# Cached attention of two blocks on one core: wq loaded in its own column order, and the permutation moved into VectorE's K transposes

## The chip, the core and the metric

The kernel runs on one core of a Trainium2 chip. The core has TensorE (PE in the profile), VectorE (DVE), ScalarE (ACT), GpSimd (POOL) and SyncE (SP), which run their own instruction streams and meet at semaphores, and sixteen DMA engines that move data between HBM and the on-chip memory SBUF. PSUM is the memory into which PE accumulates. The metric is the time of one execution in device microseconds; the runs of one kernel are told by their median.

## The reference

Two independent attention blocks, A and B, with the same shapes. Each projects x to queries, attends to a given cache of keys and values, and projects back; the two outputs stand side by side.

```python
B, Sq, D = 16, 64, 640
H, Sk, Dh = 32, 512, 128
q = (x @ wq).reshape(B, Sq, H, Dh).transpose(0, 2, 1, 3)
scores = einsum("bhqd,bhkd->bhqk", q, k_cache) * Dh ** -0.5
p = softmax(scores, axis=-1)
o = einsum("bhqk,bhkd->bhqd", p, v_cache)
out = o.transpose(0, 2, 1, 3).reshape(B, Sq, H * Dh) @ wo
```

All data are bf16. K and V are 67 MB each in a block and are read once; wq (640 x 4096) and wo (4096 x 640) are 5.2 MB each in a block.

## The kernel before

**Packs and phases.** The unit of work is a pack: 4 heads of 2 batches. A group is 4 packs (`NJ`), which share the same 2 batches and so the same x; 8 groups make a phase (32 packs), in which 16 heads go through all 16 batches. There are 4 phases: the two halves of the heads of block A, then of B; 128 packs in all. A phase needs half of a block's wq and wo: 640 x 2048 and 2048 x 640, 2.62 MB each.

**A pack n, in order of its data.** SP loads K (two DMAs of 512 KB, from pack 8 on, L631) into a ring of 6 packs and V (one of 1 MB, L641) into a ring of 4. VectorE transposes K in 32x32 blocks of 4-byte elements (KT, L702); a 4-byte element is a pair of bf16 values of neighbouring columns of a head. PE multiplies wq by x (QP, L688, 20 matmuls), ScalarE copies q (QE), PE makes the scores (S, L712), ScalarE the exponentials and their sums (EX, L741), VectorE the reciprocals (RC, L754), Pool scales (NM, four per pack, L762), PE transposes the weights (TR, L774), VectorE copies them out of PSUM (TE, L854), PE multiplies by V (PV, L867), ScalarE copies (OE), PE multiplies by wo (OP, L887). At a new group PE transposes x (XT), ScalarE copies it (XE), and Pool puts it into the one buffer that QP reads (XC, L677; in even phases also XS, L672).

**The order is planned.** `build_plan` makes a list of operations, each with its engine, a due time in units of packs (the table `AT`: QP of pack n is due at n - 0.428, S at n, and so on), and what it reads and writes. Each engine's program is its operations sorted by due time. SP's program is sorted by the times in `loads` instead. Waits follow from reads and writes: an operation waits for the last writer of what it reads, and a load for the last readers of what it overwrites. Engines run in order, so whatever stands behind a waiting operation waits too. PE's program and ScalarE's are loops, so a few waits are moved off PE: for instance QP's on its weights (where `op.kind == "QP"` in the patch-up loop, L263), and OP's on wo, which is put on the fourth NM of the pack before (L258).

**What sets SP's pace.** V of pack n goes where V of pack n - 4 was; SP takes as a sign that PV of pack n - 4 is done the TR of pack n - 3, which stands behind it on PE (`stand_in`, L294). K stands behind V in SP's order and mostly needs no wait of its own.

**wq.** Its load `LDWQ` brings, per phase, five pieces of 512 KB (one for each 128 rows; 128 partitions with runs of 4,096 bytes, L615) into a staging tile `ws_sb`. Pool copies them into `wqp_sb` with `WP` (L656), eight copies of 128 x 1280 per phase, two for each pack index j. The copies change the order of the columns: within each 512 columns pairs of columns from the two halves of a head are interleaved, so that q comes out with the head's columns in the order in which the K transpose lays K out. QP reads `wqp_sb[:, j]` in steps of four columns (`(c f) -> f c`, L685). As `ws_sb` is apart from `wqp_sb`, wq of the next phase can be loaded while this phase still computes: SP's list has the five loads for phase 1 among the first ones, and those for phases 2 and 3 spread over the phase before, 0.14 x 32 packs apart (L177). The second buffer costs 20 KB in each partition.

Of the kernel before, what the change touches and what calls it, by code (L numbers as in the profile page):

```python
# [20 lines left out]
class Cfg:  # L21
# [18 lines left out]
              TRH=(1.0, 1.05), TEH=(1.15, 1.2), TEX=1.2, PVH=(1.45, 1.46), OEH=(1.5, 1.55), OPY=(1.1, 1.57),  # L40
              OPZ=(1.65, 1.7), OSH=(1.75, 1.8), STH=(1.85, 1.9), FL1=1.3, FLM=1.68, FLC=1.82, WP0=(-1.6, -1.59, -0.7, -0.69, 0.25, 0.26, 1.25, 1.26),
              WP1=(-3.5, -2.55, -2.45, -1.5, -0.5, 0.5, 0.6, 1.5))

# [43 lines left out]
def build_plan(dims, cfg, general):  # L87
# [84 lines left out]
    for ph in range(NPH):  # L172
        twp = [ph * PH + t for t in AT["WP1" if ph else "WP0"]]
        for kt in range(dims["KT"]):
            ready = (twp[-1] - PH if ph > 1 else AT["WP0"][-1]) + 0.5
            op = add("sp", "LDWQ", (ph, kt), twp[0] - 0.5 if ph else -20.0, [], [("ws", kt, j) for j in range(NJ)])
            loads.append((ready + 2.0 + 0.14 * PH * kt if ph > 1 else AT["PV"] + 0.15 if ph else -50.0, 1, op))  # L177
        for j in range(NJ):
            w = ph * NJ + j
            n0 = ph * PH + j  # L180
            for i in range(2):
                add("pool", "WP", (w, i), twp[2 * j + i], [("ws", kt, j) for kt in range(dims["KT"])], [("wqp", j, i)])
            if ph:
                loads.append((n0 - NJ + AT["LDWO"], 4, add("sp", "LDWO", w, n0 + AT["OP"] - 0.8 * NJ, [], [("wo", j)])))
            else:
                loads.append((n0 - 1.9, 4, add("sp", "LDWO", w, n0 + AT["OP"] - 0.8 * NJ, [], [("wo", j)])))
# [6 lines left out]
    for n in range(-2, N):  # L193
# [3 lines left out]
        g, j = n // NJ, n % NJ  # L197
        add("pe", "QP", n, n + AT["QP"], [("xT", g % cfg.NX), ("wqp", j, 0), ("wqp", j, 1)], [("SB", 1)])
        add("act", "QE", n, n + AT["QE"], [], [("SB", 1), ("qs", n % cfg.NQ)])
# [53 lines left out]
    for op in ops:  # L253
# [6 lines left out]
        if op.kind == "XT" and op.idx > 0:  # L260
            at[("NM", 4 * (NJ * op.idx - NJ) + 3)].deps += [d for d in op.deps if d.kind == "LDX"]
            op.deps = [d for d in op.deps if d.kind != "LDX"]
        if op.kind == "QP" and op.idx > 0:  # L263
            op.deps = [d for d in op.deps if d.kind != "WP"]

# [15 lines left out]
    def stand_in(d, op):  # L281
# [12 lines left out]
        if d.kind == "PV" and op.eng == "sp":  # L294
            return at[("TR", d.idx + 1)]
        if d.kind == "QP" and op.eng == "pool":
            return at[("TR", d.idx - 1)]
# [28 lines left out]
    def sem_key(op):  # L326
        if op.kind == "LDX" and op.eng == "act":
            return ("d_first",) + op.writes[0]
        if op.kind == "LDV":
            return ("d_v" if op.idx[1] else "d_vh", op.writes[0][1])  # L330
        if op.kind in LOADS:
            return ("d_" + op.kind[2:].lower(),) + op.writes[0][1:]
        if op.kind in ("ST", "STH"):
            return ("d_out",)
        return ("q_" + op.eng,) if for_pe(op) else ("s_" + op.kind.lower() + "_" + op.eng,)
# [169 lines left out]
def mha_kernel(nc, blocks, out, cfg=None):  # L505
# [26 lines left out]
    with contextlib.ExitStack() as es:  # L532
# [4 lines left out]

        wqp_sb = sb("wqp_sb", [128, NJ, KT, 512], BF16)
        wo_sb = sb("wo_sb", [128, HPH, D], BF16)
        ws_sb = sb("ws_sb", [128, KT, NJ, 512], BF16)  # L540
        kn_ring = sb("kn_ring", [128, NK, 2, 2048], BF16)
# [69 lines left out]
        def em_LDWQ(e, op):  # L611
            ph, i = op.idx
            c = ph % NSUB * HPH * DH
            src = blocks[ph // NSUB][3].rearrange("(kt p) n -> p kt n", p=128)
            ins = e.dma_start(ws_sb[:, i].rearrange("p j c -> p (j c)"), src[:, i, c:c + NJ * 512])  # L615
            return ins, ins
# [34 lines left out]

        def em_WP(e, op):
            j, jj = op.idx[0] % NJ, op.idx[1]
            src = ws_sb[:, :, j].rearrange("p k (i j r) -> p k i j r", i=4, j=2)
            dst = wqp_sb[:, j].rearrange("p k (i r j two) -> p k i j r two", i=4, j=2, two=2)
            ins = e.tensor_copy(dst[:, :, :, jj], src[:, :, :, jj].rearrange("p k i (r two) -> p k i r two", two=2))  # L656
            return ins, ins

        def em_XT(e, op):
# [20 lines left out]
        def em_QP(e, op):  # L680
# [3 lines left out]
            first = last = None  # L684
            w = wqp_sb[:, j].rearrange("p k (c f) -> p k f c", f=4)  # L685
            for f in range(4):
# [11 lines left out]
        def em_KT(e, op):  # L698
            n = op.idx
            dst = kt_ring[:, n % NKT].rearrange("p t j b k two -> p (t j) b (k two)").bitcast(F32)  # L700
            src = kn_ring[:, n % NK].rearrange("p a c -> p (a c)").bitcast(F32).rearrange("p (c h b l) -> p c h b l", h=8, b=2, l=2)
            ins = e.transpose(dst.rearrange("p c b (h l) -> p c h b l", h=8, l=2), src)  # L702
            return ins, ins
# [227 lines left out]

        ahead = {}

        def units(key):
            return 16 if key[0].startswith("d_") else 1

        def emit(e, op, p, taken):
# [5 lines left out]
            for s, v in waits:  # L943
                e.wait_ge(sem[s], v * units(s))
            kind = "EXG" if p and op.kind == "EX" else op.kind
            first, last = emitters[kind](e, op)
            if last is None:
                e.sem_inc(sem[op.sem], units(op.sem))
                return
# [121 lines left out]
```

## Time and profile before

| | |
|---|---|
| median of 3 runs | 731.43 us (731.23 to 732.28) |
| the profiled execution | 732.12 us, its span 730.4 us |
| granted TensorE clock, mean | 0.99 |
| PE, weight loads, VectorE, ScalarE, Pool busy | 92%, 73%, 70%, 73%, 57% of the span |
| moved by DMA | 295.02 MB, 404 GB/s over the span |
| K transposes, L702 | 128 of 2307 ns, 295.3 us |
| Pool's NM, L762 | 508 of 695 ns, 343.4 us |
| Pool's wq copies, L656 | 32 of 1256 ns, 39.6 us |
| QP, L688 | 2560 matmuls, 165.9 us |
| wq loads, L615 | 20 of 512 KB; block A's 9.3 us from issue to landing, block B's 18.1 |

How to read it. Times are microseconds from the start of the span unless marked ns. The span is that of the program's instructions in one profiled execution; the time of that execution is 1.7 us longer. A group of instructions is told by its line in the kernel, its engine and operation, and what it writes and reads (out<-in); behind it stand busy time and the mean of one, and the idle time of the engine just before them with what ended it. SPq is SP issuing a DMA; "x5" is five in a row. "From issue to landing" is the time from the issue of a DMA to the moment its semaphore tells that all its data is there; it holds the time that the DMA stands behind others in the queue. A DMA share of 1.02 means that all sixteen engines were busy, with a little overlap between packets. Rows of a stretch give busy time and count for PE, PE's weight loads, VectorE, ScalarE and Pool in this order.

### The profile page before, as it was taken

The page shows a single profiled execution, that of the slowest core. Times are in us where ns is not written, and L with a number is a line of the kernel's source. Part 1 is how long each engine was busy: PE and PEld are TensorE (multiplying, and loading weights), DVE is VectorE, ACT ScalarE, POOL GpSimd, SP SyncE. Part 2 cuts the span into 40 slices and gives each one's busy share as a digit, 9 for nine tenths or more (in the row PEclk, how much of TensorE's full clock was granted, in tenths as well). Part 3 has the DMA queues.
Part 4 walks back from the last instruction along what each step waited for, and adds up shares of the span by engine and source line. Part 5 has one row for each costly group of instructions (what it writes and reads, how often), then busy time and mean ns, then how long its engine had stood idle before and what let it go on. Part 6 is the DMA issues. An engine that isn't in the chain of part 4 may idle for free.

```text
span 730.4 us, 61195 instructions
## 1 busy us (share of the span) xinstructions
PE 674.1 (92%) x28502; PEld 530.3 (73%) x28502; DVE 514.5 (70%) x691; ACT 533.3 (73%) x1574; POOL 417.9 (57%) x596
## 2 busy tenths in 40 slices
PE   1679999999999999999997899999999799999998
PEld 1458778787777777777775677787777577787775
DVE  5447777777777766767765667677777567878775
ACT  1447878778787777777875677777778677878775
POOL 4436565666875455554884555465587446555552
PEclk9889999999999999999999999999999999999999
DMA  8999999999999999999999999999999999999993
GB/s 337 401 404 414 414 415 413 415 414 415 415 400 409 419 414 416 416 416 417 416 411 402 415 414 413 414 415 415 414 416 407 403 415 418 417 418 417 416 415 122
DMA packets 72336, 295.02 MB, mean 404 GB/s; under 512 B 7664, under 2 KB 20080, under 8 KB 55920
## 3 DMA queue, kind: packets, MB, share of 16 engines
q1 hardware_dynamic: 72160, 294.52, 100.0%
q8 instruction: 10, 0.16, 0.1%
q10 hardware_dynamic: 144, 0.16, 0.1%
q14 instruction: 22, 0.18, 0.1%
HBM read 292.03 MB, written 2.62 MB: 403 GB/s over the span
## 4 chain that ended last, share of the span: by engine, by line
PE 53%; DMA 32%; SPq 6%; DVE 3%; issue 3%; POOL 2%; ACT 1%; DVEq 0%; POOLq 0%
DMA xn_ring<-in_B_x_dram 14%; PE ps L867 12%; PE ps L887 11%; PE ps L688 11%; PE ps L712 10%; DMA kn_ring<-in_A_k_cache_dram 9%; PE ps L774 7%; DMA kn_ring<-in_B_k_cache_dram 5%; DMA wo_sb<-in_B_wo_dram 4%; SPq L631 4%; DVE kt_ring L702 2%; POOL pn_ring L762 2%; SPq L641 1%; DVE pT_sb L854 1%; SPq L615 1%
## 5 line engine op out<-in xcount | busy, mean ns | idle before, releaser
L762 POOL TENSOR_SCALAR pn_ring<-pn_ring,recip 128x512 bf16<-128x512 bf16 x508 | 343.4, 695 | 246.1 <-DVE recip L754 221.0
L702 DVE STREAM_TRANSPOSE kt_ring<-kn_ring 128x2048 f32<-128x2048 f32 x128 | 295.3, 2307 | 120.3 <-DMA kn_ring<-in_B_k_cache_dram 80.3
L741 ACT ACTIVATE pn_ring<-ps 128x512 bf16<-128x512 f32 x512 | 296.4, 592 | 5.7 <-PE ps L712 5.7
L854 DVE COPY pT_sb<-ps 128x1024 bf16<-128x1024 bf16 x256 | 168.4, 671 | 60.2 <-PE ps L774 60.2
L688 PE MATMUL ps<-xT_ring,wqp_sb 128*128 128x128 bf16 x2560 | 165.9, 220 | 11.6 <-POOL xT_ring L677 11.6
L867 PE MATMUL ps<-pT_sb,v_ring 32*128 32x64 bf16 x16448 | 162.2, 192 | 10.6 <-DVE pT_sb L854 4.6
L688 PEld LDWEIGHTS ps<-xT_ring,wqp_sb 128*128 128x128 bf16 x2560 | 157.5, 114 | 17.8 <-issue 11.8
L867 PEld LDWEIGHTS ps<-pT_sb,v_ring 32*128 32x128 bf16 x16448 | 147.0, 91 | 24.8 <-issue 12.5
L887 PE MATMUL ps<-wo_sb,oT_sb 128*128 128x320 bf16 x1024 | 163.5, 303 | 0.0
L875 ACT ACTIVATE oT_sb<-ps 128x256 bf16<-128x256 f32 x257 | 84.7, 381 | 95.1 <-PE ps L867 95.1
L712 PE MATMUL ps<-kt_ring,qs_ring 32*64 32x512 bf16 x4096 | 138.4, 380 | 4.8 <-issue 4.8
L694 ACT ACTIVATE qs_ring<-ps 128x512 bf16<-128x512 f32 x128 | 76.4, 597 | 76.5 <-PE ps L688 74.5
L774 PEld LDWEIGHTS ps<-ident,pn_ring 64*128 64x128 bf16 x4096 | 68.3, 95 | 77.0 <-ACT oT_sb L875 46.0
L887 PEld LDWEIGHTS ps<-wo_sb,oT_sb 128*128 128x128 bf16 x1024 | 90.4, 98 | 36.7
L741 ACT ACTIVATION_READ_ACCUMULATOR pn_ring<-ps 128x1 f32 x512 | 105.3, 206 | 0.0
L774 PE MATMUL ps<-ident,pn_ring 64*128 64x64 bf16 x4096 | 82.9, 191 | 22.8 <-POOL pn_ring L762 18.6
L712 PEld LDWEIGHTS ps<-kt_ring,qs_ring 32*64 32x64 bf16 x4096 | 53.4, 103 | 32.9 <-issue 5.5
L754 DVE RECIPROCAL recip<-rowsum 128x2 f32<-128x2 f32 x256 | 40.6, 158 | 27.6 <-ACT pn_ring L741 24.6
L879 ACT ACTIVATE ps<-zeros 128x256 f32<-128x256 bf16 x128 | 49.5, 387 | 4.1
L656 POOL COPY wqp_sb<-ws_sb 128x1280 bf16<-128x1280 bf16 x32 | 39.6, 1256 | 9.9 <-DMA ws_sb<-in_A_wq_dram 6.8
L668 ACT ACTIVATE xe_sb<-ps 128x640 bf16<-128x640 bf16 x32 | 22.9, 716 | 8.7 <-PE ps L662 8.6
L677 POOL COPY xT_ring<-xe_sb 128x640 bf16<-128x640 bf16 x16 | 11.5, 717 | 21.0 <-PE ps L774 21.0
(42 smaller groups left out, 103.5 us busy)
## 6 DMA issues: line engine op xcount, KB each, us to landing
kn_ring<-in_B_k_cache_dram SPq DMA_DIRECT2D x128, 512.0 KB, 16.1
v_ring<-in_B_v_cache_dram SPq DMA_DIRECT2D x62, 1024.0 KB, 16.5
kn_ring<-in_A_k_cache_dram SPq DMA_DIRECT2D x112, 512.0 KB, 11.4
v_ring<-in_A_v_cache_dram SPq DMA_DIRECT2D x56, 1024.0 KB, 14.8
kn_ring<-in_A_k_cache_dram SPq DMA_DIRECT2D x32, 256.0 KB, 8.6
v_ring<-in_A_v_cache_dram SPq DMA_DIRECT2D x16, 512.0 KB, 8.9
ws_sb<-in_A_wq_dram SPq DMA_DIRECT2D x10, 512.0 KB, 9.3
wo_sb<-in_A_wo_dram SPq DMA_DIRECT2D x8, 640.0 KB, 13.3
```

Of the source, the lines that this page charges most:

```text
L688: last = e.matmul(ps[:, 1, f * 128:(f + 1) * 128], w[:, kt, f, :], xT_ring[:, xs, kt, :], start=(kt == 0), stop=(kt == KT - 1))
L694: ins = e.activation(qs_ring[:, op.idx % NQ].rearrange("p f b q -> p (f b q)"), ps[:, 1, :], ACTF.Copy, scale=scale)
L702: ins = e.transpose(dst.rearrange("p c b (h l) -> p c h b l", h=8, l=2), src)
L712: last = e.matmul(ps[64 * b:64 * b + 64, i, :], qs_ring[rows, n % NQ, f, b, :], kt_ring[rows, n % NKT, :, f // 2, b, :, f % 2], start=(f = ...
L741: ins = e.activation(dst, src, ACTF.Exp, scale=1.0, accum_out=sum_of(h))
L762: ins = e.tensor_scalar(pn_view(h), pn_view(h), recip[:, h:h + 1], 1.0, ALU.mult, ALU.mult)
L774: last = e.transpose(pt_bank(b)[:, 64 * c:64 * c + 64], pn[rows, c, :], ident[rows, rows], tile_position=(64 * b, 0))
L854: ins = e.tensor_copy(pT_sb[:, b].rearrange("p t q -> p (t q)"), pt_bank(b))
L867: last = e.matmul(ps[:, 4 + i, 64 * b:64 * b + 64], v_ring[rows, n % NV, b, c, :], pT_sb[rows, b, c, :], start=(t == 0 and i < 2), stop=(t ...
L875: ins = e.activation(oT_sb[:, 2 * a:2 * a + 2, :], o_ps[:, 2 * a:2 * a + 2, :], ACTF.Copy)
L879: ins = e.activation(z_ps, zeros[:, :].unsqueeze(2).broadcast_to([128, 2, 128]), ACTF.Copy)
L887: last = e.matmul(out_ps[:, s, :], oT_sb[:, i, :], wo_sb[:, 4 * j + i, s * NH0:(s + 1) * NH0], start=(j == 0 and i == 0), stop=(j == NJ - ...
```

## The change

`ws_sb` and the copies `WP` go. wq is loaded straight into `wqp_sb`, which now has the layout of wq itself (128 rows, 5 row blocks, 2048 columns).

In phase 0 there are five loads of 512 KB as before. In phases 1 to 3 there are two loads of 1.31 MB, each with half of the columns (1024, for the pack indices 0 and 1, or 2 and 3) of all five row blocks: runs of 2,048 bytes. They overwrite what the phase before reads, so they wait for its last QP that reads those columns: that of pack P - 3 for the first and of pack P - 1 for the second, P being the first pack of the phase. SP learns of it from a new semaphore that PE raises with the first matmul of the operation behind that QP (`QS`). In SP's order the loads stand at P - 4.4 and P - 2.4.

QP's wait for its weights is put on Pool again: for the first half of the columns on the XC of the phase's first group, for the second half on the fourth NM of the phase's first pack.

The order of q's columns is now that of wq, so K must be laid out to match: the transpose reads, from each run of 64 4-byte elements, first the 32 even ones and then the 32 odd ones. The order in which it writes stays.

```diff
-              ... WP0=(-1.6, -1.59, -0.7, -0.69, 0.25, 0.26, 1.25, 1.26),
-              WP1=(-3.5, -2.55, -2.45, -1.5, -0.5, 0.5, 0.6, 1.5))
+              WQ=(-3.2, -4.4))
...
-        twp = [ph * PH + t for t in AT["WP1" if ph else "WP0"]]
-        for kt in range(dims["KT"]):
-            ready = (twp[-1] - PH if ph > 1 else AT["WP0"][-1]) + 0.5
-            op = add("sp", "LDWQ", (ph, kt), twp[0] - 0.5 if ph else -20.0, [], [("ws", kt, j) for j in range(NJ)])
-            loads.append((ready + 2.0 + 0.14 * PH * kt if ph > 1 else AT["PV"] + 0.15 if ph else -50.0, 1, op))
+        for i in range(2 if ph else dims["KT"]):
+            op = add("sp", "LDWQ", (ph, i), ph * PH + 2 * i + AT["WQ"][0] if ph else -20.0, [],
+                     [("wqp", j) for j in ((2 * i, 2 * i + 1) if ph else range(NJ))])
+            loads.append((ph * PH + 2 * i + AT["WQ"][1] if ph else -50.0, 1, op))
         for j in range(NJ):
...
-            for i in range(2):
-                add("pool", "WP", (w, i), twp[2 * j + i], [("ws", kt, j) for kt in range(dims["KT"])], [("wqp", j, i)])
...
+        if j % 2:
+            add("pe", "QS", n, n + AT["QP"] + 0.001)
...
-        if op.kind == "QP" and op.idx > 0:
-            op.deps = [d for d in op.deps if d.kind != "WP"]
+        if op.kind == "QP":
+            n, j = op.idx, op.idx % NJ
+            at[("XC", n // NJ) if j < 2 else ("NM", 4 * (n - j) + 3)].deps += [d for d in op.deps if d.kind == "LDWQ"]
+            op.deps = [d for d in op.deps if d.kind != "LDWQ"]
...
+        if d.kind == "QP" and op.eng == "sp":
+            return at[("QS", d.idx | 1)]
...
-        wqp_sb = sb("wqp_sb", [128, NJ, KT, 512], BF16)
+        wqp_sb = sb("wqp_sb", [128, KT, NJ * 512], BF16)
-        ws_sb = sb("ws_sb", [128, KT, NJ, 512], BF16)
...
-            ins = e.dma_start(ws_sb[:, i].rearrange("p j c -> p (j c)"), src[:, i, c:c + NJ * 512])
+            if ph:
+                ins = e.dma_start(wqp_sb[:, :, 1024 * i:1024 * i + 1024], src[:, :, c + 1024 * i:c + 1024 * i + 1024])
+            else:
+                ins = e.dma_start(wqp_sb[:, i], src[:, i, c:c + NJ * 512])
...
-            w = wqp_sb[:, j].rearrange("p k (c f) -> p k f c", f=4)
+            w = wqp_sb[:, :, 512 * j:512 * j + 512].rearrange("p k (c f) -> p k f c", f=4)
...
-            src = kn_ring[:, n % NK].rearrange("p a c -> p (a c)").bitcast(F32).rearrange("p (c h b l) -> p c h b l", h=8, b=2, l=2)
-            ins = e.transpose(dst.rearrange("p c b (h l) -> p c h b l", h=8, l=2), src)
+            src = kn_ring[:, n % NK].rearrange("p a c -> p (a c)").bitcast(F32)
+            src = src.rearrange("p (t h b l j) -> p t j h b l", h=8, b=2, l=2, j=2)
+            ins = e.transpose(dst.rearrange("p (t j) b (h l) -> p t j h b l", j=2, h=8, l=2), src)
...
+            if op.kind == "QS":
+                marks.append(sem[op.sem])
+                return
...
+            if op.eng == "pe" and marks:
+                assert first is not last
+                first.then_inc(marks.pop(), 1)
```

More of the change, by code (lines that the diff above doesn't have):

```diff
@@ L40 @@
               TRH=(1.0, 1.05), TEH=(1.15, 1.2), TEX=1.2, PVH=(1.45, 1.46), OEH=(1.5, 1.55), OPY=(1.1, 1.57),
-              OPZ=(1.65, 1.7), OSH=(1.75, 1.8), STH=(1.85, 1.9), FL1=1.3, FLM=1.68, FLC=1.82, WP0=(-1.6, -1.59, -0.7, -0.69, 0.25, 0.26, 1.25, 1.26),
-              WP1=(-3.5, -2.55, -2.45, -1.5, -0.5, 0.5, 0.6, 1.5))
+              OPZ=(1.65, 1.7), OSH=(1.75, 1.8), STH=(1.85, 1.9), FL1=1.3, FLM=1.68, FLC=1.82,
+              WQ=(-3.2, -4.4))
 class Op:
@@ L197, in build_plan @@
         g, j = n // NJ, n % NJ
-        add("pe", "QP", n, n + AT["QP"], [("xT", g % cfg.NX), ("wqp", j, 0), ("wqp", j, 1)], [("SB", 1)])
+        add("pe", "QP", n, n + AT["QP"], [("xT", g % cfg.NX), ("wqp", j)], [("SB", 1)])
+        if j % 2:
+            add("pe", "QS", n, n + AT["QP"] + 0.001)
         add("act", "QE", n, n + AT["QE"], [], [("SB", 1), ("qs", n % cfg.NQ)])
@@ L330, in sem_key @@
             return ("d_v" if op.idx[1] else "d_vh", op.writes[0][1])
+        if op.kind == "LDWQ" and op.idx[0] == 0:
+            return ("d_wf", op.idx[1])
         if op.kind in LOADS:
@@ L650, in em_LDV @@
             return ins, ins
[L652 to L657, printed above, removed]
         def em_XT(e, op):
@@ L932, in mha_kernel @@
         ahead = {}
+        marks = []
         def units(key):
```

## The prediction

> **What bounds the kernel now.** I read the page's slices and queues first, then its chain, then busy times by stretch, then the waits, and last the order of time around the wq loads.
>
> ```profile
> DMA  8999999999999999999999999999999999999993
> GB/s 337 401 404 414 414 415 413 415 414 415 415 400 409 419 414 416 416 416 417 416 411 402 415 414 413 414 415 415 414 416 407 403 415 418 417 418 417 416 415 122
> q1 hardware_dynamic: 72160, 294.52, 100.0%
> PE 53%; DMA 32%; SPq 6%; DVE 3%; issue 3%; POOL 2%; ACT 1%; DVEq 0%; POOLq 0%
> 57.00:180.00 123.00, 123.00 (x5354) 97.41 (x5348) 96.02 (x127) 99.39 (x295) 73.64 (x109) 1.00 1.02 415
> 410.00:530.00 120.00, 113.74 (x4849) 89.66 (x4840) 84.48 (x115) 90.77 (x270) 67.19 (x100) 1.00 1.02 414
> 590.00:717.00 127.00, 126.33 (x5370) 99.97 (x5370) 97.35 (x131) 101.06 (x302) 70.23 (x104) 1.00 1.02 414
> ```
>
> The first three lines are the page's slices of DMA and its data queue, the fourth the chain by engine; the last three are stretches, with busy us of PE, its weight loads, VectorE, ScalarE and Pool, then the granted clock, DMA's share and GB/s. The sixteen DMA engines are full (share 1.02) in every stretch from about 9 to 717 us, at 414 to 418 GB/s. The span is one unbroken stream of 294.5 MB plus about 1 us of head and 13 us of tail: a microsecond in which the stream stands still, or gets longer, is a microsecond at the end, as long as PE follows it. PE follows closely. A pack (4 heads of 2 batches) costs it 5.03 us, each fourth 5.31, so 20.4 us for four, and those four bring 8.39 MB of K and V and mostly 0.16 MB of x or out, 20.6 us at 415 GB/s. In phase 0 PE never idles. From about 230 us on it waits for data:
>
> ```profile
> DVE kt_ring L702 <- DMA kn_ring<-in_B_k_cache_dram: 80.3, 64, 2.8
> POOL pn_ring L762 <- DMA wo_sb<-in_B_wo_dram: 15.1, 7, 2.5
> SPq L641 <- PE ps L774: 251.1, 105, 4.5
> ```
>
> The third line says how the stream is fed: SP waits for a TR (L774) that frees a V slot, then issues one V and one K. What keeps DMA busy meanwhile is the queue already issued. In phase 0 that queue is short, and wq for phase 1 is a part of it:
>
> ```profile
> 40.00 0.59 SPq L608 DMA_DIRECT2D xn_ring<-in_A_x_dram  x1
> 40.63 2.33 SPq L615 DMA_DIRECT2D ws_sb<-in_A_wq_dram  x5
> 46.05 0.80 SPq L646 DMA_DIRECT2D v_ring<-in_A_v_cache_dram  x2
> 46.89 2.38 SPq L629 DMA_DIRECT2D kn_ring<-in_A_k_cache_dram  x4
> 53.81 0.81 SPq L646 DMA_DIRECT2D v_ring<-in_A_v_cache_dram  x2
> ...
> DMA to landing us min/median/max: 8.7/8.7/8.7
> ...
> DMA to landing us min/median/max: 12.5/12.5/12.5
> ```
>
> The last two lines are the x load issued at 40.00 and the fifth wq load, issued at 42.54. They land at 48.68 and 55.03: wq fills 6.35 us of the stream.
>
> **The change, part by part.**
>
> *Pool's copies go*: 32 by 1256 ns, 40 us of a Pool busy 57%. At the start the XC copy stood behind two of them and can run at 12.2 instead of 14.6, with the first QP 2.4 us earlier. But the next PE work, PV at 18.38, waited 0.60 us for VectorE's pT memsets, which stand behind the first K transpose (14.83, when its K landed). So the start gains nothing: 0. At the phase starts the copies cost PE about 0.6 us (QP of packs 33 to 36 take 20.98 us, not 20.4); where the stream decides, this is hidden: 0. Without that cover it is rival 2.
>
> *2 KB runs.* wq of phases 1 to 3 now comes in two loads of 128x5 runs of 2,048 B instead of five of 4,096 B runs. In the trace's packet records a 4,096 B packet took 163.1 ns (34,816 of them), a 2,048 B one 86.5 ns (1,024, of the last four V loads). Per phase 1,280 x 86.5/16 = 6.92 us against 640 x 163.1/16 = 6.52: +0.4, three times: **+1.2 us**. (Bounds: the 2,048 B median of 84 ns gives +0.6; the rate of the 1,280 B packets, 57.6 ns each, which are 22.2 bytes a ns, gives 7.37 us or +2.5.) Larger loads could also be cheaper per byte: the page "DMA: Bandwidth & Descriptors" of the Trainium skill (section "Anatomy of one DMA") puts about 2 us of fixed cost on each DMA, by which nine wq loads fewer (11, not 20) would be an estimated 18 us less. The trace disagrees here: the five wq loads at 40.63 landed 1.26 us apart, which is 512 KB at 415 GB/s with no fixed cost between them.
>
> *The load moves.* wq has no second buffer now, so its load waits for the last readers: columns 0 to 1023 wait for QP of pack P-3 (P the phase's first pack), the rest for QP of P-1. For phase 1 it leaves 40 us and goes to about 184 us, and the stream of phase 0 loses 6.35 us of work.
>
> (a) After x, in at 48.68, the V and K issued at 46.05 keep it going until 53.7. The next issue, 53.81, waits for a TR that PE's own start sets (stalls for "issue" of 4.8 and 4.0 us), so I leave it there. By the packet records data starts 1.4 us after an issue (0.93 to 2.37) and landing is told 0.5 us after the last packet. So DMA stands still from 53.2 to 55.2: 2.0 us. After that each issue comes as the queue runs out (period 5.1 us, work 5.15).
>
> (b) At 181 us the second gap:
>
> ```profile
> 181.29 0.37 SPq L641 DMA_DIRECT2D v_ring<-in_A_v_cache_dram  x1
> 182.29 1.28 PE L688 MATMUL ps<-xT_ring,wqp_sb 128*128 128x128 bf16 x20
> 183.50 1.21 PE L867 MATMUL ps<-pT_sb,v_ring 32*128 32x64 bf16 x128
> ...
> DMA to landing us min/median/max: 11.2/11.2/11.2
> ```
>
> SP issued V at 181.29. Now the wq load stands ahead of it and waits for the QP of pack 29, told by the first matmul of the PV behind it: about 183.7. Queued behind are that V, its K, then all loads. Data starts at 185.1. The last line is the last K issued before (177.26): it landed at 188.43, so its data was in at 187.9, and with 6.35 us less in the stream it is in at 181.6. The stream is late by 185.1 - 181.6 = **3.5 us**, (a) and (b) together, however they are divided. Bounds: 0 if PE is 3.5 us earlier; 5.9 if the 2.4 us of SP's delay come on top.
>
> The V itself is needed some 16 us later: free. wq lands near 189 and 202 us, ahead of its readers in Pool's order (XC of group 8 at about 196.6, the last NM of pack 32 at about 205): no stall there. Late next are the four wo loads behind wq: they hold PE back until it is as late as the stream.
>
> In the later phases the queue is 16 to 18 us long (issue to landing), so wq lands about 17 us after its wait: XC and the last NM, and every NM behind them on Pool, wait for it. By the same arithmetic QP of pack 64 comes about 2 us and of pack 66 about 6 us later than before. The queue goes on during that and loses only as much length, so I take **0**. The cover is that before, too, PE lost 7.9 us to the wo loads right behind (QP of packs 67 to 70: 7.07, 6.88, 6.83, 7.51), and wo lands when the stream says. Without cover: rival 3. The wq loads no longer spread over phases 1 and 2 come back at the boundary, 6.3 us each way: 0.
>
> *K's transposes* read 32 elements 8 bytes apart. No row reads so on VectorE. Its own writes go in pairs of 4 bytes to places 64 bytes apart and it takes 2307 ns for 2048 elements; PE's weight loads with an 8-byte step (L688) take 114 ns against 98 for dense ones (L887), 16% more. So 0 to +0.37 us each; a memset of 4096 elements in 3.47 us would allow -0.57, which only adds idle time. In phase 0 there is room:
>
> ```profile
> 132.44 2.29 DVE L702 STREAM_TRANSPOSE kt_ring<-kn_ring 128x2048 f32<-128x2048 f32 x1
> 135.47 0.69 DVE L854 COPY pT_sb<-ps 128x1024 bf16<-128x1024 bf16 x1 [0.74 <-PE ps L774]
> ```
>
> 0.74 us between transpose and the copy that PE waits for. In the later phases the transpose starts when K lands, and +0.37 would be paid once. I take 0, by its own write side. The Trainium skill, "SBUF — State Buffer", section "Door 1: The DMA port swizzle", says that SBUF is read in lines of 16 bytes and wants at least two hits on each; an 8-byte step gives just two, so by it +0, by the weight-load row +0.37 us in all.
>
> **Sum**: 3.5 + 1.2 = **+4.7 us**. The profiled execution, 732.12 us (span 730.4 and 1.7 around it), would take 736.8; it is 0.7 above the median of the three runs, 731.43, so I forecast **736.1 us**.
>
> **Rivals.**
>
> 1. *The queue does not run dry* (PE's start is earlier, SP further ahead). Only the 2 KB runs remain: 732.6 us, no change to measure. For it: PE's stall of 4.0 us at 41.3 falls where the five wq loads are issued, and these go. Against: PV at 18.38 and the chain behind it do not depend on Pool.
>
> 2. *Faster: PE's chain, not the stream, sets the end.* The chain of waits gives PE 53% and DMA 32%, and names Pool's copy at the phase starts. If K's landing has slack, 0.6 to 0.9 us at each of three boundaries come off and nothing is paid: 731.4 - 2.2 = 729.2 us. It decides if DMA's engines have room that the 1.02 hides. Against: 120 us of K waits, and a rate that falls only where packets are small. Another way to faster is that each load costs time of its own: the first x load, 160 KB alone, took 2.28 us to land, some 1.9 of it not data; nine loads fewer would give 17 us, 719. The 1.26 us spacing speaks against it.
>
> 3. *wq's waits are not given back.* Behind the last boundary PE can catch up little: from QP of pack 102 to that of 127 it took 129.3 us, and 25 packs cost at least 127.5. If the 6 us of packs 64 to 66 and 96 to 98 come on top of the stream's lateness, the two give up to 12 less 1.8 to 4: 742 to 746.
>
> 4. *The strided read halves VectorE's rate.* A transpose of 4.6 us makes a pack on VectorE 4.6 + 1.34 + 0.32 = 6.3 us, more than PE's 5.1: 128 x 6.3 = 806 plus about 25 of head and tail, 830 us.
>
> **How the numbers follow.** Forecast 57%, rival 1 13%, rival 2 9% and its second way 1%, rival 3 13%, rival 4 4%; 3% for slower ways that I don't see. The measurement tells 0.2%, 1.46 us, from no change. Faster is rival 2 in both ways: 0.10. Same is rival 1: 0.13. The rest is slower: 0.77. The forecast's own range is 732.6 (no idle) to 738.5 (SP's delay on top). For 8 in 10 I add rival 1 below, to 731.0, and the nearer half of rival 3 above, to 742.5.
>
> **What would show it.** Right: two dips of DMA's share below 1, near 54 and 184 us, 3 to 4 us in all, and 3,840 more packets of 2,048 B; V issued near 184 and not 181; POOL waiting for wqp loads at L677 and L762 near packs 64 and 96; QP of pack 100 some 4 to 5 us later than 572.6; transposes near 2.3 us. Wrong: no dip at all (rival 1), a dip near 550 or PE short of data at the end (rival 3), a span below 729.

## The result and the profile after

The changed kernel takes 739.48 us, the median of four runs (738.74 to 739.62); beside them the kernel before took 731.33 (731.18 to 732.28). The ratio is 1.0107, 95% interval 1.0089 to 1.0124: slower by about 8 us. The profiled execution took 739.62 us, its span 737.9, 7.5 more than before.

First the page of the changed kernel: slices of DMA, its data queue, the chain by engine, the K transposes and block B's late wq loads.

```profile
DMA  8989999999999999999999999999999999999993
GB/s 336 402 325 379 416 414 415 416 412 417 381 406 405 416 417 416 415 417 415 411 409 403 411 412 415 415 413 415 415 411 407 400 414 417 415 419 416 416 415 125
...
q1 hardware_dynamic: 73936, 294.52, 99.5%
...
PE 69%; DMA 19%; SPq 5%; issue 2%; DVE 2%; ACT 1%; POOL 1%; POOLq 0%; DVEq 0%
...
L703 DVE STREAM_TRANSPOSE kt_ring<-kn_ring 128x2048 f32<-128x2048 f32 x128 | 295.4, 2307 | 115.3 <-DMA kn_ring<-in_B_k_cache_dram 74.0
...
wqp_sb<-in_B_wq_dram SPq DMA_DIRECT2D x4, 1280.0 KB, 16.1
```

The same bytes, 294.52 MB, go through the queue; one thing is new: the third and fourth slices (37 to 74 us) carry 325 and 379 GB/s, where the kernel before carried 404 and 414. The chain's shares moved from DMA to PE, though PE got no new work (its busy time is 676.8 us). That is a warning about the chain: it names who was last at each step, and in a kernel whose stream and PE are nearly as long as each other this flips with little. Transposes cost what they did, 2307 ns.

The stretches around the dip, with busy time and count of PE, its weight loads, VectorE, ScalarE and Pool, then clock, DMA's share and GB/s. Before:

```profile
45.00:50.00 5.00, 4.76 (x49) 3.75 (x49) 3.63 (x5) 0.00 (x0) 2.70 (x4) 0.50 1.01 400
50.00:55.00 5.00, 4.58 (x208) 3.31 (x207) 1.12 (x3) 3.29 (x11) 0.89 (x2) 0.94 1.03 410
55.00:60.00 5.00, 5.00 (x222) 4.09 (x220) 3.63 (x6) 3.80 (x13) 2.53 (x4) 1.00 1.02 413
...
185.00:190.00 5.00, 5.00 (x233) 4.01 (x219) 4.21 (x7) 4.37 (x13) 4.72 (x7) 1.00 1.01 411
```

After:

```profile
45.00:50.00 5.00, 3.81 (x45) 3.00 (x45) 3.21 (x5) 0.00 (x0) 2.35 (x4) 0.69 0.69 244
50.00:55.00 5.00, 5.00 (x216) 3.89 (x215) 1.78 (x4) 3.53 (x11) 1.47 (x3) 0.97 0.82 302
55.00:60.00 5.00, 5.00 (x221) 3.88 (x219) 3.64 (x6) 3.81 (x13) 2.52 (x5) 1.00 0.75 276
60.00:120.00 60.00, 60.00 (x2646) 47.50 (x2643) 46.52 (x61) 48.18 (x143) 36.20 (x54) 1.00 1.02 413
185.00:190.00 5.00, 5.00 (x220) 3.96 (x206) 4.18 (x7) 4.57 (x13) 2.05 (x4) 1.00 0.94 303
```

By GB/s the stretch of 45 to 60 us moved (400 - 244 + 410 - 302 + 413 - 276) x 5 us = 2.0 MB less, 4.9 us of a stream of 412 GB/s. By the share it stood still for only 4.0 us: (1.02 - 0.69 + 1.02 - 0.82 + 1.02 - 0.75) x 5. The rest is in the packets: of those started in 45 to 60 us a 4,096 B packet took 188.5 ns in the mean, against 163.1 in the kernel before. By the packet records this is no general slowness. 38 of those 512 packets took 265 to 1,015 ns, and they bunch where the stream starts again (47.7 to 49.1, 54.5 to 55.1 and 56.3 to 57.4 us); the other 474 took 160.4 ns. From 60 us on the stream is full again, and PE has no idle time. At 185 us there is a second dip: 0.4 us by the share, but (411 - 303) x 5 us = 0.54 MB or 1.3 us by bytes. Some 0.3 us of that are the 2 KB runs of the wq load that starts there.

The loss is then paid elsewhere. These are PE's QP of pack 32, pack 37 and pack 38 in the changed kernel's timeline (start, length), and Pool's normalizations that PE waits for, with the idle time before each:

```profile
197.88 1.28 PE L688 MATMUL ps<-xT_ring,wqp_sb 128*128 128x128 bf16 x20
...
211.75 0.69 POOL L763 TENSOR_SCALAR pn_ring<-pn_ring,recip 128x512 bf16<-128x512 bf16 x1 [1.15 <-DMA wo_sb<-in_A_wo_dram]
218.60 0.69 POOL L763 TENSOR_SCALAR pn_ring<-pn_ring,recip 128x512 bf16<-128x512 bf16 x1 [2.45 <-DMA wo_sb<-in_A_wo_dram]
225.46 0.69 POOL L763 TENSOR_SCALAR pn_ring<-pn_ring,recip 128x512 bf16<-128x512 bf16 x1 [2.45 <-DMA wo_sb<-in_A_wo_dram]
227.97 1.28 PE L688 MATMUL ps<-xT_ring,wqp_sb 128*128 128x128 bf16 x20
232.32 0.69 POOL L763 TENSOR_SCALAR pn_ring<-pn_ring,recip 128x512 bf16<-128x512 bf16 x1 [2.46 <-DMA wo_sb<-in_A_wo_dram]
235.11 1.28 PE L688 MATMUL ps<-xT_ring,wqp_sb 128*128 128x128 bf16 x20
```

Before, the QP of packs 32 and 37 started at 197.66 and 223.67, and that of pack 38 so:

```profile
229.07 1.28 PE L688 MATMUL ps<-xT_ring,wqp_sb 128*128 128x128 bf16 x20
```

Up to pack 32 PE is level with the kernel before (+0.22 us), 140 us after the dip. Then it waits for the four wo loads of phase 1, which come as late as the stream is, and at pack 38 it is 6.04 us late. So most of the time is lost at 45 to 60 us, which sets PE back by next to nothing at that point, and is seen at 210 to 235 us.

PE's lateness against the kernel before, by the start of QP (us), in the changed kernel and in two of the experiments below:

| pack | 32 | 36 | 38 | 50 | 62 | 66 | 77 | 93 | 98 | 127 |
|---|---|---|---|---|---|---|---|---|---|---|
| changed kernel | +0.2 | +2.5 | +6.0 | +3.8 | +0.4 | +8.5 | +5.6 | +1.1 | +7.4 | +7.6 |

| pack | 32 | 36 | 38 | 50 | 62 | 68 | 76 | 92 | 100 | 127 |
|---|---|---|---|---|---|---|---|---|---|---|
| late_ph1 | -0.1 | +2.7 | +6.2 | +6.8 | +6.8 | +6.9 | +7.2 | +7.0 | +7.0 | +7.0 |
| late_ph23 | +0.7 | +0.6 | +0.8 | -1.8 | -6.0 | +0.1 | -0.1 | -5.5 | +0.8 | +1.0 |

### The profile page after: what moved, and what is told of

It is laid out like the page before. It is cut to its first block, busy times and chain, and to the rows that moved or that the text cites. A ratio compares the mean times of both kernels' runs of the same rounds, so it can differ in the third digit from the quotient of the medians.

```text
span 737.9 us, 61147 instructions
## 1 busy us (share of the span) xinstructions
PE 676.8 (92%) x28502; PEld 531.6 (72%) x28502; DVE 517.3 (70%) x691; ACT 532.8 (72%) x1574; POOL 378.3 (51%) x564
## 3 DMA queue, kind: packets, MB, share of 16 engines
q1 hardware_dynamic: 73936, 294.52, 99.5%
HBM read 292.03 MB, written 2.62 MB: 399 GB/s over the span
## 4 chain that ended last, share of the span: by engine, by line
PE 69%; DMA 19%; SPq 5%; issue 2%; DVE 2%; ACT 1%; POOL 1%; POOLq 0%; DVEq 0%
PE ps L868 16%; PE ps L888 16%; PE ps L688 15%; PE ps L713 13%; PE ps L775 8%; DMA xn_ring<-in_B_x_dram 7%; DMA kn_ring<-in_A_k_cache_dram 4%; SPq L638 3%; DMA kn_ring<-in_B_k_cache_dram 2%; DMA wqp_sb<-in_B_wq_dram 2%; DMA wo_sb<-in_B_wo_dram 2%; DMA wo_sb<-in_A_wo_dram 2%; SPq L648 1%; PE ps L662 1%; DVE kt_ring L703 1%
## 5 line engine op out<-in xcount | busy, mean ns | idle before, releaser
L703 DVE STREAM_TRANSPOSE kt_ring<-kn_ring 128x2048 f32<-128x2048 f32 x128 | 295.4, 2307 | 115.3 <-DMA kn_ring<-in_B_k_cache_dram 74.0
L677 POOL COPY xT_ring<-xs_sb 128x640 bf16<-128x640 bf16 x16 | 11.5, 716 | 22.4 <-PE ps L775 19.9
```

The source lines that it names most:

```text
L703: ins = e.transpose(dst.rearrange("p (t j) b (h l) -> p t j h b l", j=2, h=8, l=2), src)
```

## The experiments

Eleven kernels were timed, each with runs of the kernel before on the same chip. In the table "us" is the median, "ratio" that to the kernel before (731.9 to 732.0 us in every group), with its 95% interval.

| kernel | wq of phase 1 | wq of phases 2, 3 | us | ratio |
|---|---|---|---|---|
| staged_4k | early, staged | early, staged | 732.56 | 1.0007 (0.9998 to 1.0015) |
| staged_2k | early, staged, 2 KB runs | early, staged, 2 KB runs | 733.1 | 1.0014 (1.0005 to 1.0023) |
| late_ph1 | late, straight | early, staged | 738.91 | 1.0089 (1.0076 to 1.0102) |
| late_ph23 | early, staged | late, straight | 732.96 | 1.0015 (1.0006 to 1.0024) |
| late_filled | late, straight; 2.62 MB unread at pack 1 | late, straight | 739.72 | 1.0113 (1.0094 to 1.0132) |
| late_klead35 | late, straight; K one pack earlier | late, straight | 738.55 | 1.0090 (1.0075 to 1.0105) |
| staged_p16 | staged, loaded at pack 16 | early, staged | 738.99 | 1.0087 (1.0074 to 1.0100) |
| kstock8 | late, straight; up to 2 more K packs in stock | late, straight | 736.46 | 1.0059 (1.0046 to 1.0072) |
| kstock6 | late, straight; 1 more K pack in stock | late, straight | 737.08 | 1.0071 (1.0058 to 1.0084) |
| kstock8_sooner | kstock8, asked for sooner | late, straight | 735.04 | 1.0042 (1.0029 to 1.0056) |
| late_filled_p16 | late, straight; 2.62 MB unread at pack 16 | late, straight | 745.0 | 1.0178 (1.0164 to 1.0192) |

The theory at first was the prediction's: a stream that stands still for 3.5 us, in two places, and longer runs. Rivals were that the strided transposes, the new start or the 2 KB runs cost the time, or the waits of the later phases.

**Which part, and which phase.** These four kernels are built from the changed one. Its K transposes, wq's own column order and the straight load in phase 0 stay; a phase that is not "late" gets the staging tile back, early loads and plain copies on Pool (no change of order). Per phase LATE and HALF (two loads with 2 KB runs) are set; for staged_4k:

```diff
+    LATE = (True, False, False, False)
+    HALF = (False, False, False, False)
...
+                op = add("sp", "LDWQ", (ph, i), ph * PH - 4.0, [], [("ws", i, j) for j in js])
+                loads.append((ph * PH - 28.0 + 0.14 * PH * kt if ph > 1 else AT["PV"] + 0.15, 1, op))
+        if not cfg.LATE[ph]:
+            for j in range(NJ):
+                for a in range(2):
+                    add("pool", "WP", (ph * NJ + j, a), ph * PH + AT["WP1"][2 * j + a],
+                        [("ws", i, j) for i in range(2 if two else dims["KT"])], [("wqp", j, a)])
...
+        ws_sb = sb("ws_sb", [128, KT, NJ * 512], BF16)
...
+        def em_WP(e, op):
+            c = 512 * (op.idx[0] % NJ) + 256 * op.idx[1]
+            ins = e.tensor_copy(wqp_sb[:, :, c:c + 256], ws_sb[:, :, c:c + 256])
```

The others differ in the flags: staged_2k has HALF (False, True, True, True); late_ph1 has LATE (True, True, False, False) and HALF (False, True, False, False); late_ph23 has LATE (True, False, True, True) and HALF (False, False, True, True).

staged_4k:

> Keeps the staging for phases 1 to 3, with the five loads of 4 KB runs at their old places in SP's order, and Pool's copies, which now copy without reordering; K's transposes read every second element, and phase 0 is loaded straight, as in the changed kernel. Theory (the DMA stream sets the end; what it loses is the gap in phase 0 and the 2 KB runs): both are gone, so 731.3 us within 0.7, no dip of DMA's share after 10 us, transposes 2.31 us. Rival (the strided read or the new start costs): 733 or more, with the transposes above 2.35 us or the dip at 45 to 60 us still there.

staged_2k:

> As staged_4k, but wq of phases 1 to 3 comes in two loads of 1.31 MB with runs of 2,048 bytes, still early and into the staging tile. Theory: the runs alone. By the packet records of the kernel before (86.5 ns) +1.2 us over staged_4k, by those of the changed kernel (89.9 ns, (1280 x 89.9 - 640 x 163.7) / 16 = 0.64 us a phase) +1.9: 732.5 to 733.3. Rival (the runs cost nothing, or hold up what is around them): 731.3, or above 735.

late_ph1:

> Phase 1 has its wq straight and late, as in the changed kernel; phases 2 and 3 have it staged and early, as before. Theory: the whole gap in phase 0 (4.3 us by the changed kernel's DMA share) and one phase of 2 KB runs (0.64): +4.9, 736.2 us, with the dips at 45 to 60 and near 185 us. Rival (the waits for wq at packs 64 and 96 are the larger part): about +2.7 or less, 734 at most.

late_ph23:

> The other half: phase 1 staged and early, phases 2 and 3 straight and late. Theory: two phases of 2 KB runs, +1.3, 732.6 us, though PE waits about 6 us more at pack 66 and at pack 98. Rival (these waits are not given back): +5 or more, 736.5 us or above; by a sum of parts late_ph1 and late_ph23 together make the 8.15 us of the changed kernel.

staged_4k takes 0.07% more than before, and its interval holds 1: the strided transposes, the column order and the new start cost nothing that can be told. late_ph1 has nearly the whole loss (0.89 of 1.07%) and late_ph23 next to nothing. The table of lateness shows why the later phases are free: in late_ph23 PE gains 6 us within a phase, because the next phase's wq is no longer spread over it, and hands them back at the boundary. But late_ph1 came out 2.7 us above the 736.2 expected: one moved load, with its 2 KB runs, costs 738.91 - 732.56 = 6.35 us by the medians (6.0 by the two ratios), and not 3.5 plus a little. So the place of the loss was right and its size was not.

**Filling the hole.** late_filled is the changed kernel with five loads of 512 KB (wq again, into a tile that nobody reads) at the old place:

```diff
+        if ph == 1:
+            for i in range(dims["KT"]):
+                loads.append((AT["PV"] + 0.15, 1, add("sp", "LDWQ", (ph, 10 + i), ph * PH - 4.0, [], [("ws", i, 0)])))
```

> The changed kernel with one thing added: at the old place of phase 1's wq in SP's order (issued near 40 us) the five loads of 512 KB run as well, into a tile that nothing reads, 2.62 MB more for the stream. Theory: 4.3 us of DMA's time stand idle in phase 0 and take most of it, so only 6.35 - 4.3 = 2.0 us show: 741.5 us, with no dip left. Rival (the end is set otherwise, and the stream was no shorter for the gap): the full 6.35 us, 745.8, or nothing, 739.5.

late_klead35 lets all K loads be issued one pack earlier:

```diff
-    KLEAD = 2.5
+    KLEAD = 3.5
```

> The changed kernel with one number changed: K's place in SP's order is one pack earlier (KLEAD 3.5 for 2.5; the ring of six allows it). Theory: one pack of K, 1.05 MB or 2.5 us of stream, is queued ahead all the time, so the gap in phase 0 shrinks from 4.3 to 1.8 us: 737.0 us. Rival (the gap does not set the time): 739.5, or later because V lands behind more K: above 740.

Both went against the theory as it stood: late_filled took the rival's time, and late_klead35, at 738.55, lies between the two and cannot be told from the changed kernel by the intervals. The stretches of late_filled, columns as above:

```profile
45.00:50.00 5.00, 4.27 (x66) 3.17 (x69) 3.40 (x5) 0.02 (x1) 2.54 (x4) 0.66 1.02 403
50.00:55.00 5.00, 3.58 (x198) 2.58 (x191) 0.87 (x2) 2.79 (x9) 0.84 (x2) 1.00 1.03 410
55.00:60.00 5.00, 5.00 (x222) 3.96 (x220) 3.79 (x6) 3.95 (x14) 2.74 (x5) 1.00 1.02 412
```

The hole is full, with 2.62 MB (6.35 us) more in the stream, and the time is the same, 739.72. Bytes explain what the share did not. Added up from the packet records (all queues, a packet under way counted in part), at 210 us the kernel before had moved 85.06 MB, the changed one 82.43, and late_filled 84.80, of which 82.18 are of use: 0.25 MB or 0.6 us behind the changed kernel. What I had taken for 4.0 us of idle time is worth 4.9 in bytes, and with the 1.3 of the dip at 185 us the hole is almost as long as the load that left it.

In late_klead35 most of the hole is gone too:

```profile
45.00:50.00 5.00, 4.76 (x114) 3.66 (x114) 3.63 (x5) 0.42 (x1) 2.69 (x4) 0.66 1.03 400
50.00:55.00 5.00, 4.77 (x191) 3.60 (x181) 1.82 (x5) 3.56 (x12) 1.99 (x3) 1.00 0.90 355
```

At 210 us it had moved 1.35 MB more than the changed kernel, and still its QP of pack 38 came 6.2 us after that of the kernel before, as late as in the changed kernel. The extra bytes are a pack of K that stays ahead to the end, and the wo loads that PE waits for stand behind it in the queue. So bytes help only if they stand ahead of what PE waits for; that is my reading of this trace, and the reason why the kernels with K in stock below give the lead back.

That gave the theory its second form. In phase 0 every ring slot is filled as soon as it is free, so what may be loaded is set by PE; the stream can hold more only near 45 to 60 us. There a phase's wq is free. Anywhere later in phase 0 it costs its own length. The rival: what costs is the late load itself, that is its wait for the QP of pack 29, its place just ahead of wo, its going straight into place.

**Place alone.** staged_p16 has no late load at all. It is staged_4k with phase 1's early loads at pack 16:

```diff
-                loads.append((ph * PH - 28.0 + 0.14 * PH * kt if ph > 1 else AT["PV"] + 0.15, 1, op))
+                loads.append((ph * PH - 28.0 + 0.14 * PH * kt if ph > 1 else 16.0, 1, op))
```

> staged_4k (staging tile, 4 KB runs, plain copies by GpSimd, ratio 1.0007) with one thing changed: the five wq loads of phase 1 are issued at pack 16 and not at pack 1. Theory, in its second form: from the third pack to the 33rd PE takes a pack each 5.03 us and every ring slot is filled as soon as it is free, so the stream can run ahead only near 45 to 60 us; the 2.62 MB of a phase's wq (6.35 us of the stream at 412 GB/s) are free there and nowhere later. So: the DMA share dips near 50 us as in the changed kernel, packs from 38 on start some 6 us later, and the time is 6.35 x (5.0 of 6.35 idle, plus what is lost later) = about +6 over staged_4k: 738.2, 736.8 to 739.0. Rival, that what costs is the late load itself (its wait for QP of pack 29, its landing just before the wo loads, its going straight into the place): nothing of that is in this kernel, so 732.6, as staged_4k.

It takes 738.99 us, 6.4 more than staged_4k by the medians (5.9 by the two ratios), and has the hole:

```profile
45.00:50.00 5.00, 3.28 (x35) 2.23 (x35) 2.40 (x5) 0.00 (x0) 1.54 (x3) 0.50 0.52 172
50.00:55.00 5.00, 5.00 (x214) 4.05 (x213) 1.59 (x2) 2.53 (x7) 1.56 (x3) 0.87 0.90 314
55.00:60.00 5.00, 4.99 (x220) 3.92 (x218) 3.53 (x6) 3.69 (x13) 3.02 (x5) 1.00 0.92 301
60.00:120.00 60.00, 60.00 (x2609) 47.71 (x2613) 47.19 (x63) 48.25 (x145) 36.55 (x54) 1.00 1.01 407
185.00:190.00 5.00, 5.00 (x221) 4.01 (x205) 4.19 (x7) 4.35 (x13) 4.70 (x7) 1.00 1.03 418
```

The last row has the full stream at 185 us, where this kernel's SP has no QP to wait for, and PE is still 6.6 us late at pack 38. So the rival is not needed for the loss: with staging, 4 KB runs and no wait for a QP, the place by itself costs some 6 us.

late_filled_p16 asks the same of the filler, which moves to pack 16:

```diff
-                loads.append((AT["PV"] + 0.15, 1, add("sp", "LDWQ", (ph, 10 + i), ph * PH - 4.0, [], [("ws", i, 0)])))
+                loads.append((16.0, 1, add("sp", "LDWQ", (ph, 10 + i), ph * PH - 4.0, [], [("ws", i, 0)])))
```

> late_filled with one thing changed: its five unread loads (2.62 MB) lie at pack 16 and not at pack 1. Theory, second form: in late_filled they lay in idle time and cost 0.2 us; at pack 16 the stream has no idle time, the dip near 50 us stays as in the changed kernel, and the loads add their 6.35 us: 745.5, 744 to 746.5. Rival, that PE sets the pace all through phase 0 and leaves room for 2.62 MB anywhere in it: 739.5 to 740.

745.0 us, 5.3 more than with the filler at pack 1 by the medians, 4.8 by the ratios (the profiled execution was the fastest of its five, 742.82). The same loads are free at 40 us and cost three quarters or more of their length at pack 16. Whether the idle stretch near 45 us holds more than these 2.62 MB was not measured.

**Filling the hole with something of use.** kstock8 puts two K slots where the staging tile was and lets K run up to two packs further ahead in phase 0; the lead goes back while wq and wo of phase 1 are loaded. kstock6 does it by one pack in the six slots there are, with 1.0, 6 and 33 for 2.0, 6 and 34:

```diff
-    NK = 6
+    NK = 8
...
-                loads.append((n - cfg.NV + AT["PV"] + 0.2 - cfg.KLEAD, 2, op))
+                loads.append((n - cfg.NV + AT["PV"] + 0.2 - cfg.KLEAD - max(0, min(2.0, 0.45 * (n - 6), 2.0 - 0.45 * (n - 34))), 2, op))
```

> The changed kernel (wq late and straight into its place) with two more K slots in the room that the staging tile leaves (NK 8 for 6), and K loaded up to two packs earlier: the lead grows by two from pack 6 to 11, so that two K packs more (2.1 MB) are loaded near 45 to 60 us, and goes back by two over the K loads of packs 34 to 39, where wq and wo of phase 1 come. Theory, second form: the idle time is used by K in place of wq; the dip near 50 us goes, at packs 38 to 40 PE is behind the kernel before by 1 to 2 us and not 6, and of the 8.1 us over it about 5 go: 734.5, 733.3 to 736.0. Rival, that the late load itself costs: no change, 739.5.

kstock6:

> As kstock8, with one pack and the six K slots there are (lead 3.5 from pack 9, back to 2.5 over the K loads of packs 33 to 36): 1.05 MB more in the idle time, 2.5 us. Theory, second form: 737.0, 736.2 to 738.0, better than a lead of 3.5 kept to the end (late_klead35, ratio 1.0090), since there the stock is never used up at the crossing. Rival, that the late load itself costs: 739.5.

kstock6 came out as expected, and better than the lead kept to the end (737.08 against 738.55, though the two intervals overlap). kstock8 missed its range: it won only 3.5 of the 5 us (0.48% by the ratios of the changed kernel and of kstock8), and its own stretch tells why:

```profile
45.00:50.00 5.00, 4.50 (x46) 3.49 (x46) 3.62 (x5) 0.00 (x0) 2.69 (x4) 0.50 0.79 295
```

By bytes nearly half of the hole was still there (at 60 us 0.96 MB behind the kernel before, the changed one 2.05): the K loads stood behind the V load at which SP waits. kstock8_sooner asks for them ahead of it (and gives the lead back faster):

```diff
-                loads.append((n - cfg.NV + AT["PV"] + 0.2 - cfg.KLEAD - max(0, min(2.0, 0.45 * (n - 6), 2.0 - 0.45 * (n - 34))), 2, op))
+                loads.append((n - cfg.NV + AT["PV"] + 0.2 - cfg.KLEAD - max(0, min(2.0, 0.8 * (n - 5), 2.0 - 0.8 * (n - 34))), 2, op))
```

> kstock8 with the two extra K packs asked for sooner (the lead grows by 1.6 to 2 from pack 7 on), so that they are in SP's order ahead of the V load at which the stream stands still near 46 us. kstock8's trace still showed the dip (DMA share 0.805 in 45 to 50 us, 0.962 in 50 to 55; 1.5 us in all). Theory, second form: the dip goes and with it those 1.5 us: ratio to before 1.0059 - 1.5/731.9 = 1.0038, 1.0025 to 1.0055; what is left is the 2 KB runs (some 1.9 us) and under 1 us. Rival, that kstock8's rest is the late load itself (wait on QP, place before wo): 1.0059 again, whatever the dip does.

```profile
45.00:50.00 5.00, 4.55 (x47) 3.54 (x47) 3.63 (x5) 0.00 (x0) 2.70 (x4) 0.50 1.05 399
50.00:55.00 5.00, 4.63 (x204) 3.41 (x203) 0.64 (x1) 2.81 (x9) 0.68 (x1) 0.84 1.04 415
55.00:60.00 5.00, 5.00 (x221) 3.96 (x219) 3.66 (x6) 3.83 (x13) 2.74 (x5) 1.00 1.00 390
...
185.00:190.00 5.00, 5.00 (x211) 3.92 (x198) 4.19 (x7) 4.24 (x14) 2.07 (x4) 1.00 0.87 298
```

The hole is gone, the ratio is 1.0042, and at pack 38 PE is 2.1 us late and not 6.0. So of the 1.07% that the change cost, 0.65 came back by filling the hole, with wq still late and straight. What is left can be read by bytes: against the kernel before it is 0.06 MB ahead at 60 us, 0.23 behind at 185, 0.76 at 190 and 1.33 at 700, which is 3.2 us of stream for a span 3.4 us longer. The step at 185 to 190, 1.3 us, lies at the late load's own place, where SP waits for a QP and the first 2 KB runs come, so that much of the rival stands. No version beat the kernel before; its stream is full from about 9 us to 717, and each experiment only moves bytes within it.

## Why the prediction was right, and where its sizes were off

The direction and the mechanism held: the stream stands still where wq left it, and PE pays when the wo loads come late. The size did not: 4.7 us were forecast and some 8 measured, so the median came out 3.4 us above the forecast. It lies in the range of 731.0 to 742.5, but above the forecast's own 732.6 to 738.5, in the part that was added for rival 3; and rival 3 did not happen. That the range held is in part luck. By its own steps:

*The standing still* was mis-sized: 3.5 us in the sum, some 6 us by bytes (5.0 by 60 us, and 1.3 near 185 us less 0.3 for the 2 KB runs). The step that failed is in (a), "After x, in at 48.68, the V and K issued at 46.05 keep it going until 53.7". I took x's landing for the moment at which the queue ahead of wq is done. In the changed kernel, us by us:

```profile
44.00:45.00 1.00, 0.00 (x0) 0.00 (x0) 0.00 (x0) 0.27 (x2) 0.00 (x0) 1.00 1.01 391
45.00:46.00 1.00, 0.00 (x0) 0.00 (x0) 0.00 (x0) 0.00 (x0) 0.00 (x0) 1.00 0.73 289
46.00:47.00 1.00, 0.81 (x25) 0.68 (x25) 0.21 (x1) 0.00 (x0) 0.00 (x0) 0.95 0.44 178
47.00:48.00 1.00, 1.00 (x6) 0.54 (x5) 1.00 (x3) 0.00 (x0) 0.35 (x1) 0.50 0.62 96
48.00:49.00 1.00, 1.00 (x8) 0.77 (x7) 1.00 (x3) 0.00 (x0) 1.00 (x3) 0.50 0.65 237
...
54.00:55.00 1.00, 1.00 (x14) 0.84 (x12) 1.00 (x3) 1.00 (x5) 0.73 (x2) 1.00 0.49 86
...
58.00:59.00 1.00, 1.00 (x43) 0.81 (x36) 0.18 (x1) 1.00 (x4) 0.00 (x0) 1.00 0.55 225
```

The queue began to run dry near 45 us, some 3 us before the landing on which I built; at 46 to 47 us more than half of the engines' time was idle, and the next issue came at 46.72. A landing is told when the last part of a DMA is done. In the trace of the kernel before, the semaphore of that x load rises in sixteen steps, half of them by 46.46 us and the last at 48.68; the first of the sixteen steps of the wq load behind it comes at 46.80, ahead of x's landing. So before 48.68 us most engines were already at wq, and without wq they had nothing to do. Nor did the stream catch up at once: the issues of 53.57 and 58.74 each came too late again (the last two rows), where the text has "After that each issue comes as the queue runs out".

With 5.0 us lost at the first hole, "3.5 us, (a) and (b) together, however they are divided" could not hold: the stream cannot be less late than its first hole made it. The second hole came on top. SP issued wq at 183.90, as predicted (183.7), and the dip there was 1.0 us by bytes without the 2 KB runs, where the sum left 1.5. Its reckoning in (b) starts from a landing again, that of the K issued at 177.26.

```profile
40.48 0.58 SPq L612 DMA_DIRECT2D xn_ring<-in_A_x_dram  x1
46.72 0.81 SPq L653 DMA_DIRECT2D v_ring<-in_A_v_cache_dram  x2
47.57 3.45 SPq L636 DMA_DIRECT2D kn_ring<-in_A_k_cache_dram  x4
53.57 1.42 SPq L653 DMA_DIRECT2D v_ring<-in_A_v_cache_dram  x2
...
183.90 0.37 SPq L620 DMA_DIRECT2D wqp_sb<-in_A_wq_dram  x1
```

*The 2 KB runs* were put at 1.2 us (bounds 0.6 to 2.5). The 3,840 more packets came. Over the whole kernel a 2,048 B packet took 89.9 ns in the mean, not 86.5, but that is two things. In the full stream the wq packets took 88.0 to 88.5 ns, late (changed kernel) or early (staged_2k); the first wq load behind the dip at 185 us alone took 102.5 (median 84), with 57 of its 640 packets over 150 ns. So the runs cost (1,280 x 88.1 - 640 x 163.3)/16 = 0.5 us for each phase, 1.5 in all, and not the 1.9 that 89.9 ns give. As time, staged_2k against staged_4k shows 0.5 us with intervals of about 0.6 us on each side; the runs do not settle where between 0.5 and 1.5 it lies.

*The sum*, by bytes: the changed kernel is 2.05 MB behind the kernel before at 60 us, 2.65 at 190 and 3.14 at 700, which is 5.0, 6.4 and 7.6 us at 412 GB/s, for a span that grew by 7.5.

*Who is late next*: "Late next are the four wo loads behind wq: they hold PE back until it is as late as the stream" is what Pool's four waits and packs 36 to 38 show.

*Later phases* taken as 0: right, late_ph23 (732.96) and the table of lateness show it. The waits are there: XC's before packs 64 and 96, that of the fourth NM before pack 98 only. Near pack 66 the same NM waited 3.84 us, by the profile for a load of x.

```profile
POOL xT_ring L677 <- DMA wqp_sb<-in_B_wq_dram: 5.3, 2, 2.7
POOL pn_ring L763 <- DMA wqp_sb<-in_B_wq_dram: 3.4, 1, 3.4
```

QP of pack 64 came 2.2 us later, as predicted. That of pack 66 came 8.5 us later, 2 us more than the predicted 6 and the 0.4 that was left at pack 62; by pack 67 it was 6.9, so it was given back as argued. QP of pack 100 came at 580.11, 7.5 us later and not 4 to 5: that is the mis-sized stream again.

*The start* at 0: right. The first QP came 1.74 us earlier (13.74 us), but the first K transpose began at 16.02 us and not at 14.83, when its K landed, so QP of pack 1 came 2.1 us later; by pack 2, behind PE's stalls for "issue", it was 0.3. *K's transposes* at 0: right, 2307 ns before and after. The page "SBUF — State Buffer" of the Trainium skill, section "Door 1: The DMA port swizzle", by which an 8-byte step still gives two hits on each line of 16 bytes, agrees with that number; the weight loads' row, 16% more for a strided read, did not carry over to VectorE.

*Rivals.* 1 (the queue does not run dry) did not happen. The stall that was to go with the five wq issues was still there, and no shorter (4.0 us before):

```profile
46.19 0.50 PE L775 MATMUL ps<-ident,pn_ring 64*128 64x64 bf16 x22 [4.36 <-issue]
```

2 (PE's chain sets the end) is refuted by staged_p16 and late_filled_p16, in which PE's work is unchanged and bytes alone move the end. Its second way, a cost of each load, is refuted by staged_2k: nine loads fewer than staged_4k, and the time did not fall (+0.5 us). The page "DMA: Bandwidth & Descriptors" of the Trainium skill, section "Anatomy of one DMA — SWDGE (gpsimd) path", puts about 2 us of fixed cost on each DMA of that path, most of it completion latency. The loads here are issued from SP, and behind others in a full queue none of it shows in this run. 3 is refuted by late_ph23, 4 by the transposes' row.

## What to carry to other kernels

In a kernel that is one full stream, ask of each early load what stretch it fills. A load that lies where the stream would be idle was free here. Moved from there into a full stretch (pack 16, or the boundary) it cost three quarters of its length or more, however well its own wait is hidden; moved from one full stretch to another (late_ph23) it cost next to nothing. Such a loss shows far from its cause, here 150 us later as waits for other loads, so compare bytes moved up to a given time, not idle time, between the two traces, and ask whether the bytes stand ahead of what the computing engines wait for. To find when a queue is empty, look at the share of the engines and not at the landing of its last load. If buffer space is won by such a change, spend it on what can be loaded into the hole: two K slots and an earlier place in the issuing order won back 0.65 of 1.07%.

## What the hardware showed unexpectedly

- The time from issue to landing is no measure of when the queue ahead is empty. Before, an x load of 160 KB landed at 48.68 us; without wq behind it, DMA's share was down to 0.73 at 45 to 46 us. In the changed kernel the sixteen steps of x's semaphore lie between 45.54 and 48.79 us, nine of them before 46.6 and seven from 47.41 on. The share at 46 to 47 us, 0.44 or seven of sixteen, fits that. Why the parts of one load end 3 us apart was not tried.
- A queue that runs dry costs more than the share of its engines says: 4.0 us of idle share were 4.9 us of bytes. The difference lies in the packets with which the stream starts again: 38 of 512 took 265 to 1,015 ns, the rest 160.4. Why these take so long was not tried.
- The same shows in the 2,048 B packets of wq: 88.0 to 88.5 ns in the full stream, late or early, but 102.5 in the mean (median 84) in the one load behind a dip.
